# Moving parts of the weight decoding of a windowed attention + FFN kernel from ScalarE and VectorE to GpSimd

## The chip, the cores and the metric

One core of one Trainium2 chip. The metric is the device time of one execution in microseconds; three executions of the kernel before gave 1013.37, 1012.92 and 1012.87 us (median 1012.92).

## What is computed

An attention over 8 batches and 8 heads (512 local tokens that see a window of 32 to each side and 32 global tokens that see everything; head dimension 64), whose output of 4608 x 512 goes through a feed-forward layer (512 to 2048 to 512). Everything is float32.

```
s_ll = scale * q_l @ k_l^T, masked to |i - j| <= 32
a_l  = softmax([scale * q_l @ k_g^T, s_ll]);   out_l = a_l @ [v_g, v_l]
out_g = softmax(scale * q_g @ [k_g, k_l]^T) @ [v_g, v_l]
x = rows of [out_g, out_l], heads side by side (4608 x 512)
h = x @ w_in;  r = max(h, 0);  g = s * (r * r) + b;  out = g @ w_out
```

## The kernel before

Matrix products are made of split numbers: an operand m is cut into a high part `hi` (m rounded to float32r) and a low part `lo = m - hi`, and three float32r products (hi hi, hi lo, lo hi) are summed. ScalarE mostly makes the high part (a cast), VectorE or GpSimd the low part (a subtraction).

The program is one loop over steps j. Step j does one head-half of the attention, `scores` (or `scores32`, the unsplit form of the first 16 steps), softmax, transposes and the product with v; and, ten steps behind (LAG), one piece of the feed-forward layer: `ffn_in` (L517: 24 matmuls of 256 columns into `ps_h`; then Relu on ScalarE, L523, and squaring on VectorE, L524; then g's high part on ScalarE, L531, and its low part on VectorE, L532) and a step later `ffn_out` (L549: 12 matmuls of 512 columns into `acc`). There are 128 attention steps and 136 feed-forward pieces.

The two weight matrices come as 16 chunks, both matrices together 2 x 1024 numbers per partition for a chunk: `weight_load` brings chunk k as 64-bit integers (the bits of float64 numbers, 2 x 512 KB, tile `wst`), and `weight_chunk` decodes it at step k into `w_all`, by halves: the first half is columns 0 to 511 (w_in's), the second 512 to 1023 (w_out's). For each half `weight_words` (L152 on) issues six instructions of 512 columns on 128 partitions: ScalarE takes the upper bits of the low word (L160, tile `wup`) and the scaled high word (L161); VectorE shifts (L164) and adds (L165), which gives the float32 number m in `wst`; ScalarE casts it to the high part (L168), and VectorE subtracts for the low part (L169). Feed-forward piece m reads chunks 2 (m mod 8) and the one behind it, so the last chunk is wanted at step 17. After that the weights stay in `w_all` for the whole run. `wst` has four buffers, shared with other tiles (tags xs0, xs1 and two of kq); chunk k's buffer is loaded again, or used as `kq` or `xs`, when both low parts of the chunk that was there have been made.

Each engine works through its instructions in order. That order isn't the order of the code: a scheduler lays all instructions out beforehand by its own estimates of their lengths, so an edit at one place can move instructions everywhere. Loads go out in order on SyncE's queue. GpSimd has no decoding to do before the change: in the first 93 us it makes the masks and one small tile (`qgs`, L366), and from then on the low parts of q, v and of every other k (L206, L214, L204, L461).

Of the kernel before, what the change touches and what calls it, by code (L numbers as in the profile page):

```python
# [65 lines left out]
def f32(ap):  # L66
    return ap.bitcast(F32)
# [3 lines left out]
def window_attention_then_ffn(ctx: ExitStack, tc: tile.TileContext, qd, qg, kw, vw, vg, qz, qgz, vz, w_in, w_out, sv, bv, out):  # L71
    nc = tc.nc
# [37 lines left out]
    for tile_, c0, shift in ((mask_low, 32, -32), (mask_mid, 32, 0), (mask_high, 0, 32)):  # L110
        nc.gpsimd.memset(tile_, 0.0)
        part = tile_[:, c0:c0 + 192]
        for sign, base in ((1, -shift), (-1, 64 + shift)):
            nc.gpsimd.affine_select(
                out=part, in_=part, pattern=[[sign, 192]], compare_op=ALU.is_ge,
# [31 lines left out]
    def weight_chunk(k):  # L147
        st = staged.pop(k)
        n = 2 if k < BY_HALVES else 1
        for i in range(n):  # L150
            c = 1024 // n
            weight_words(k, st[:, 2 * c * i:2 * c * (i + 1)], slice(c * i, c * (i + 1)))  # L152

    def weight_words(k, st, at):
        words = st.rearrange("p (n w) -> p n w", w=2)
        low, high = words[:, :, 0], words[:, :, 1]
        n = at.stop - at.start
        pool, tag = ((ops, "vsg"), (sb, "pg"))[(k + at.start // 512) % 2]
        up = pool.tile([P, n], I32, tag=tag, name=f"wup{k}_{at.start}", bufs=1)
        nc.scalar.activation(out=up, in_=low.bitcast(U32), func=AF.Copy, scale=2.0**-29)  # L160
        nc.scalar.activation(  # L161
            out=low.bitcast(F32), in_=high.bitcast(F32), func=AF.Prelu, scale=2.0**-112, alpha=2.0**32,
        )
        nc.vector.tensor_scalar(out=low, in0=low, scalar1=3, scalar2=None, op0=ALU.logical_shift_left)  # L164
        nc.vector.tensor_tensor(out=low, in0=low, in1=up, op=ALU.add)  # L165
        m = low.bitcast(F32)
        hi, lo = (w_all[:, i, k].rearrange("p w c -> p (w c)")[:, at] for i in range(2))
        nc.scalar.copy(out=hi, in_=m)  # L168
        nc.vector.tensor_sub(out=lo, in0=m, in1=f32(hi))  # L169


    NS = B * 2 * H
# [426 lines left out]
    for j in range(NM + LAG + 2):  # L599
# [27 lines left out]
        m = j - LAG if LAG <= j < NM + LAG else None  # L627
# [91 lines left out]
```

## Time and profile before

| | before |
|---|---|
| median of 3 executions | 1012.92 us |
| the profiled execution | 1013.71 us, span of its trace 1011.9 us |
| TensorE busy | 996.1 us (98%) |
| VectorE busy | 809.4 us (80%) |
| ScalarE busy | 707.6 us (70%) |
| GpSimd busy | 289.4 us (29%) |
| mean granted TensorE clock | 0.997 of 2.4 GHz |

In the traces PE is TensorE's matmuls, PEld its weight loads, DVE VectorE, ACT ScalarE, POOL GpSimd, SP SyncE. The matmuls are pipelined and their ends modelled, so a full PE column says that matmuls followed one another, not that TensorE was at its peak. A row of grouped instructions gives the busy time and the mean of one, and behind the bar the engine's idle time before them with what ended it.

### The profile page before, as it was taken

The numbers are of one execution on the slowest core, as the hardware profiler recorded it, in microseconds if no ns is written. First come the engines' busy times: TensorE is split into PE (matmuls) and PEld (weight loads), VectorE is DVE, ScalarE is ACT, GpSimd is POOL, SyncE is SP. The second block draws the span as 40 slices with busy tenths as digits, with TensorE's granted clock in tenths as the row PEclk, the third lists the DMA queues.
The fourth block names the chain that finished last, engine by engine and source line by source line (L and its number), as shares of the span: only waits on it lengthen the run. The fifth ranks groups of instructions, "written<-read, shape, count | busy, mean of one in ns | idle before, by whom it ended". The sixth has DMA issues, their size and how long they took to land.

```text
span 1011.9 us, 20076 instructions
## 1 busy us (share of the span) xinstructions
PE 996.1 (98%) x6946; PEld 906.9 (90%) x6948; DVE 809.4 (80%) x2111; ACT 707.6 (70%) x1817; POOL 289.4 (29%) x366
## 2 busy tenths in 40 slices
PE   9799999999999999999999999999999999999998
PEld 5599899999999999999999999999999999999887
DVE  6999879988789788888789779988799788964322
ACT  7999767868677667868677667867678667743222
POOL 1001433424244224424234223424234223401000
PEclk9999999999999999999999999999999999999999
DMA  9765312313122212313132112312132112101000
GB/s 327 266 229 182 98 48 63 108 34 96 47 88 69 65 48 62 97 42 90 47 99 69 54 59 62 97 42 87 44 104 70 53 55 65 62 1 49 23 22 21
DMA packets 63557, 82.05 MB, mean 81 GB/s; under 512 B 7648, under 2 KB 50656, under 8 KB 63456
## 3 DMA queue, kind: packets, MB, share of 16 engines
q1 hardware_dynamic: 63168, 79.72, 25.2%
q8 instruction: 55, 0.90, 0.4%
q10 hardware_dynamic: 288, 1.05, 0.3%
q14 instruction: 46, 0.38, 0.1%
HBM read 71.30 MB, written 9.44 MB: 80 GB/s over the span
## 4 chain that ended last, share of the span: by engine, by line
PE 91%; ACT 5%; DVE 2%; DMA 1%; issue 0%
PE ps_h L517 35%; PE acc L549 35%; PE ps_s L375 5%; PE ps_o L403 4%; PE turned L311 3%; PE turned L313 3%; PE ps_og L469 2%; PE ps_g L382 1%; PE warm L105 1%; DMA rk<-in_kw 1%; ACT wst L161 1%; ACT wup L160 1%; ACT w_all L168 1%; ACT sm L231 1%; PE turned L447 1%; PE ps_s L286 1%
## 5 line engine op out<-in xcount | busy, mean ns | idle before, releaser
L517 PE MATMUL ps_h<-xst,w_all 128*128 128x256 f32 x3264 | 437.5, 281 | 1.8 <-ACT xst L502 0.7
L549 PE MATMUL acc<-w_all,g 128*128 128x512 f32 x1632 | 422.0, 396 | 0.0
L517 PEld LDWEIGHTS ps_h<-xst,w_all 128*128 128x128 f32 x3264 | 407.6, 189 | 9.3 <-ACT xst L489 1.1
L549 PEld LDWEIGHTS acc<-w_all,g 128*128 128x128 f32 x1632 | 289.8, 188 | 49.8
L214 POOL TENSOR_TENSOR vs<-rv,vs 128x192 fp32r<-128x192 f32 x112 | 70.7, 631 | 291.0 <-ACT vs L213 289.9
L524 DVE SCALAR_TENSOR_TENSOR r<-ps_h,s_t,r 128x512 f32<-128x512 f32 x136 | 101.4, 746 | 53.7 <-ACT r L523 52.2
L231 ACT ACTIVATE sm<-sm,nm 128x224 f32<-128x224 f32 x256 | 121.5, 478 | 32.5 <-DVE nm L225 31.3
L206 POOL TENSOR_TENSOR kq<-rq,kq 128x256 fp32r<-128x256 f32 x112 | 92.8, 828 | 169.2 <-ACT kq L205 160.3
L532 DVE SCALAR_TENSOR_TENSOR g<-r,b_t,g 128x512 fp32r<-128x512 f32 x136 | 112.0, 824 | 35.6 <-ACT g L531 31.1
L531 ACT ACTIVATE g<-r,b_t 128x512 fp32r<-128x512 f32 x136 | 98.6, 725 | 52.0 <-DVE r L524 51.9
L523 ACT ACTIVATE r<-ps_h 128x512 f32<-128x512 f32 x136 | 81.3, 598 | 67.7 <-PE ps_h L517 58.4
L241 DVE TENSOR_SCALAR sm<-sm,nm 128x224 f32<-128x224 f32 x256 | 92.2, 402 | 3.9
L461 POOL TENSOR_TENSOR vsg<-rvg,vsg 128x320 fp32r<-128x320 f32 x64 | 56.9, 910 | 107.1 <-ACT vsg L460 107.1
L375 PE MATMUL ps_s<-kq 128*128 128x224 f32 x448 | 73.7, 275 | 2.3 <-DVE nm L225 2.3
L375 PEld LDWEIGHTS ps_s<-kq 128*128 128x128 f32 x448 | 67.3, 190 | 8.9 <-ACT pt L328 2.5
L392 ACT CAST pt<-turned 128x416 fp32r<-128x416 f32 x112 | 57.5, 514 | 23.5 <-PE turned L313 22.8
L393 DVE TENSOR_TENSOR pt<-turned,pt 128x416 fp32r<-128x416 f32 x112 | 65.4, 584 | 6.9 <-ACT pt L392 6.2
L386 ACT COPY tg<-ps_g 32x256 f32<-32x256 f32 (+1 forms) x112 | 42.2, 377 | 33.9 <-PE ps_g L382 31.4
L387 DVE TENSOR_TENSOR sg<-ps_g,tg 32x256 f32<-32x256 f32 (+1 forms) x112 | 48.2, 430 | 20.7 <-ACT tg L386 15.9
L311 PE MATMUL turned<-ident,sm 128*96 128x128 f32 (+1 forms) x256 | 63.9, 274 | 0.0
L313 PE MATMUL turned<-ident,sm 128*128 128x128 f32 x256 | 63.2, 273 | 0.0
L403 PE MATMUL ps_o<-pt,vs 128*128 128x256 f32 x336 | 62.6, 295 | 0.0
(79 smaller groups left out, 1288.0 us busy)
## 6 DMA issues: line engine op xcount, KB each, us to landing
rq<-in_qd SPq DMA_DIRECT2D x112, 128.0 KB, 2.1
rk<-in_kw SPq DMA_DIRECT2D x64, 176.0 KB, 2.3
rv<-in_vw SPq DMA_DIRECT2D x112, 96.0 KB, 1.9
rvg<-in_vg SPq DMA_DIRECT2D x32, 320.0 KB, 3.0
out<-o SPq DMA_DIRECT2D x34, 256.0 KB, 2.2
wst<-in_w_in SPq DMA_DIRECT2D x15, 512.0 KB, 4.4
wst<-in_w_out SPq DMA_DIRECT2D x15, 512.0 KB, 5.5
rv<-in_vz SPq DMA_DIRECT2D x16, 192.0 KB, 4.2
```

The costliest lines, as they stand in the source:

```text
L206: nc.gpsimd.tensor_sub(out=qs[:, 1, :], in0=rq, in1=f32(qs[:, 0, :]))
L231: nc.scalar.activation(out=p, in_=p, func=AF.Exp, bias=nm[:, blk:blk + 1], scale=-1.0, accum_out=ss[:, blk:blk + 1],)
L241: nc.vector.tensor_scalar(out=p, in0=p, scalar1=ss[:, blk:blk + 1], scalar2=1.0, op0=ALU.mult, op1=ALU.mult,)
L311: nc.tensor.transpose(out=p_t[0:n, s0:s0 + P], in_=sm[:, c0:c0 + n], identity=ident)
L313: nc.tensor.transpose(out=p_t[:, o0:o0 + P], in_=sm[:, c0:c0 + P], identity=ident)
L375: nc.tensor.matmul(p_s[:, W * blk:W * blk + W], lhsT=qs[:, a, blk * P:(blk + 1) * P], rhs=ks[:, KEYS[blk]], start=(a == 0), stop=(a == 1),)
L403: nc.tensor.matmul(p_o[:, :, q], lhsT=vs[0:n, c], rhs=pt[0:n, :, o], start=(c == 0), stop=(c == 1))
L517: nc.tensor.matmul(p_h[:, k], lhsT=wi[:, a, f, c], rhs=xs[:, e, c, :], start=(n == 0), stop=(n == 11),)
L524: nc.vector.scalar_tensor_tensor(out=r, in0=p_h, scalar=s_t, in1=r, op0=ALU.mult, op1=ALU.mult)
L531: nc.scalar.activation(out=g[:, 0], in_=r, func=AF.Identity, bias=b_t)
L532: nc.vector.scalar_tensor_tensor(out=g[:, 1], in0=r, scalar=b_t, in1=f32(g[:, 0]), op0=ALU.add, op1=ALU.subtract,)
L549: nc.tensor.matmul(oacc[t][i], lhsT=g[:, a, k, i * P:(i + 1) * P], rhs=wo[:, e, f, :], start=(pr == 0 and n == 0), stop=(pr == 7 and n == 5),)
```

## The change

In `weight_words` the first half of every chunk (`at.start` is 0) has its high part made by GpSimd (`tensor_copy`) in place of ScalarE, and its low part by VectorE as before; the second half has its high part made by ScalarE as before and its low part by GpSimd in place of VectorE. So 16 of the 32 casts leave ScalarE, 16 of the 32 subtractions leave VectorE, and GpSimd gets 32 instructions of 128 x 512.

```diff
         m = low.bitcast(F32)
         hi, lo = (w_all[:, i, k].rearrange("p w c -> p (w c)")[:, at] for i in range(2))
-        nc.scalar.copy(out=hi, in_=m)
-        nc.vector.tensor_sub(out=lo, in0=m, in1=f32(hi))
+        if not at.start:
+            nc.gpsimd.tensor_copy(out=hi, in_=m)
+        else:
+            nc.scalar.copy(out=hi, in_=m)
+        (nc.gpsimd if at.start else nc.vector).tensor_sub(out=lo, in0=m, in1=f32(hi))
```

Line numbers behind the edit grow by 3: the copy on GpSimd is L169, the cast on ScalarE L171, both subtractions L172, and what was L206, L225, L524 is L209, L228, L527.

GpSimd's order. In each row stands the operation, the tile written and the tiles read. Before, behind the masks (L114), the first things that it does are `qgs` and the low parts for step 16:

```order
L114 AFFINE_SELECT mask_high_63<-mask_high_63 128x192
L366 TENSOR_TENSOR qgs1_1134<-rqg1_1032,qgs1_1134 128x8x32
L206 TENSOR_TENSOR kq16_1097<-rq16_1016,kq16_1097 128x256
L204 TENSOR_TENSOR kq16_1097<-rk16_1014,kq16_1097 64x352
L206 TENSOR_TENSOR kq16_1097<-rq17_1102,kq16_1097 128x256
```

With the change the 32 decoding instructions stand ahead of and among these; the rows for chunks 11 to 15 (CAST is the copy of a first half, TENSOR_TENSOR on `w_all` the subtraction of a second half):

```order
L169 CAST w_all_60<-wst11_601 128x512
L172 TENSOR_TENSOR w_all_60<-wst11_601,w_all_60 128x512
L172 TENSOR_TENSOR w_all_60<-wst12_664,w_all_60 128x512
L169 CAST w_all_60<-wst12_664 128x512
L169 CAST w_all_60<-wst13_735 128x512
L172 TENSOR_TENSOR w_all_60<-wst13_735,w_all_60 128x512
L172 TENSOR_TENSOR w_all_60<-wst14_833,w_all_60 128x512
L169 CAST w_all_60<-wst14_833 128x512
L209 TENSOR_TENSOR kq16_1097<-rq16_1016,kq16_1097 128x256
L207 TENSOR_TENSOR kq16_1097<-rk16_1014,kq16_1097 64x352
L209 TENSOR_TENSOR kq16_1097<-rq17_1102,kq16_1097 128x256
L169 CAST w_all_60<-wst15_915 128x512
```

Two subtractions or two copies now follow each other, and the low parts for step 16 stand between those of chunks 14 and 15.

VectorE's order around chunk 12 (`wst12`); ISA on `wst` is the addition (L165), ISA on `sm` the masked row maximum of the softmax. Before:

```order
L164 TENSOR_SCALAR wst12_664<-wst12_664 128x512
L234 TENSOR_SCALAR nm15_1124<-nm15_1124 128x2
L165 ISA wst12_664<-wst12_664,wup12_512_843 128x512x2
L235 RECIPROCAL nm15_1124<-nm15_1124 128x2
L169 TENSOR_TENSOR w_all_60<-wst11_601,w_all_60 128x512
L241 TENSOR_SCALAR sm15_1123<-sm15_1123,nm15_1124 128x224 x2
L524 SCALAR_TENSOR_TENSOR r4_1072<-ps_h4_1047,s_t_90,r4_1072 128x512
L169 TENSOR_TENSOR w_all_60<-wst12_664,w_all_60 128x512
L164 TENSOR_SCALAR wst12_664<-wst12_664 128x512
L165 ISA wst12_664<-wst12_664,wup12_0_836 128x512x2
L532 SCALAR_TENSOR_TENSOR g4_1075<-r4_1072,b_t_91,g4_1075 128x512
```

With the change:

```order
L164 TENSOR_SCALAR wst12_664<-wst12_664 128x512
L165 ISA wst12_664<-wst12_664,wup12_0_836 128x512x2
L527 SCALAR_TENSOR_TENSOR r3_973<-ps_h3_948,s_t_90,r3_973 128x512
L237 TENSOR_SCALAR nm14_1038<-nm14_1038 128x2
L238 RECIPROCAL nm14_1038<-nm14_1038 128x2
L244 TENSOR_SCALAR sm14_1037<-sm14_1037,nm14_1038 128x224 x2
L164 TENSOR_SCALAR wst13_735<-wst13_735 128x512
L172 TENSOR_TENSOR w_all_60<-wst12_664,w_all_60 128x512
```

One subtraction for each chunk is left, and between the addition that feeds GpSimd's copy and the subtraction that reads the copy the scheduler has put five other rows (six instructions).

SyncE's order of loads, from chunk 4's on, before:

```order
L265 DMA rk4_243<-in_kw 128x352
L271 DMA rq4_245<-in_qz 128x256
L145 DMA wst4_247<-in_w_in 128x1024
L145 DMA wst4_247<-in_w_out 128x1024
L271 DMA rq5_292<-in_qz 128x256
```

With the change the two loads of chunk 4, which also wait for GpSimd now (it releases the buffer), stand ahead of step 4's keys and queries:

```order
L145 DMA wst4_247<-in_w_in 128x1024
L145 DMA wst4_247<-in_w_out 128x1024
L268 DMA rk4_243<-in_kw 128x352
L274 DMA rq4_245<-in_qz 128x256
L274 DMA rq5_292<-in_qz 128x256
```

## Rows read from the trace of the kernel before

**Rows 1.** The page: the span; busy time, share and instructions of each engine.

```profile
span 1011.9 us, 20076 instructions
PE 996.1 (98%) x6946; PEld 906.9 (90%) x6948; DVE 809.4 (80%) x2111; ACT 707.6 (70%) x1817; POOL 289.4 (29%) x366
```

**Rows 2.** Busy time of each engine by stretch: the stretch (us), its length, then busy us (and instructions) of PE, PEld, DVE, ACT, POOL; granted clock, DMA share, GB/s.

```profile
24.00:52.00 28.00, 22.06 (x130) 16.59 (x131) 26.31 (x92) 27.39 (x69) 0.00 (x0) 1.00 0.78 265
52.00:96.00 44.00, 44.00 (x300) 40.42 (x300) 42.30 (x108) 43.69 (x99) 3.24 (x4) 1.00 0.66 223
96.00:108.00 12.00, 9.45 (x62) 8.29 (x61) 11.87 (x26) 11.03 (x27) 5.64 (x8) 1.00 0.26 76
108.00:200.00 92.00, 92.00 (x659) 85.59 (x660) 79.24 (x208) 68.22 (x183) 34.61 (x42) 0.98 0.26 79
```

**Rows 3.** The same for 24 to 108 us in one piece.

```profile
24.00:108.00 84.00, 75.51 (x489) 65.30 (x490) 80.47 (x224) 82.10 (x193) 8.89 (x11) 1.00 0.64 216
```

**Rows 4.** Pieces of the chain that ended last, 86 to 100 us: start, us on the chain, engine, tile, line.

```profile
86.27 0.54 ACT w_all L168
...
90.85 0.58 ACT wst L161
...
95.93 0.75 DVE w_all L169
```

**Rows 5.** Waits in 24 to 108 us: the waiting engine, tile and line, what it waited for, us in total, times, longest.

```profile
PE ps_s L375 <- DVE nm L225: 2.3, 1, 2.3
...
DVE w_all L169 <- ACT w_all L168: 0.2, 1, 0.2
```

**Rows 6.** VectorE's largest groups that read nothing but SBUF, in 24 to 108 us, and ScalarE's casts of the decoding: count | busy us, mean ns | idle before.

```profile
L169 DVE TENSOR_TENSOR w_all<-wst,w_all 128x512 fp32r<-128x512 f32 x27 | 18.8, 702 | 0.3 <-ACT w_all L168 0.2
L165 DVE CUSTOM_DVE_ANT_0 wst<-wst,wup 128x1024 uint16<-128x1024 uint16 x26 | 18.5, 713 | 0.2
L164 DVE TENSOR_SCALAR wst<-wst 128x512 int32<-128x512 int32 x25 | 10.6, 425 | 1.6 <-ACT wst L161 1.1
L241 DVE TENSOR_SCALAR sm<-sm,nm 128x224 f32<-128x224 f32 x28 | 9.5, 381 | 0.0
...
L532 DVE SCALAR_TENSOR_TENSOR g<-r,b_t,g 128x512 fp32r<-128x512 f32 x7 | 5.2, 748 | 0.4 <-ACT g L531 0.2
...
L168 ACT CAST w_all<-wst 128x512 fp32r<-128x512 f32 x26 | 17.3, 666 | 0.4 <-DVE wst L165 0.3
```

**Rows 7.** Two successive instructions on VectorE in order of time: start, length in us.

```profile
101.55 0.68 DVE L169 TENSOR_TENSOR w_all<-wst,w_all 128x512 fp32r<-128x512 f32 x1
102.15 0.69 DVE L165 CUSTOM_DVE_ANT_0 wst<-wst,wup 128x1024 uint16<-128x1024 uint16 x1
```

**Rows 8.** GpSimd's subtractions over the whole run: count, duration in ns least/median/greatest, first and last start.

```profile
L214 POOL TENSOR_TENSOR vs<-rv,vs x112: 589/602/1056, 99.4 to 894.9; 128x192 fp32r<-128x192 f32 x112
...
L206 POOL TENSOR_TENSOR kq<-rq,kq x112: 724/741/1313, 93.3 to 876.3; 128x256 fp32r<-128x256 f32 x112
...
L461 POOL TENSOR_TENSOR vsg<-rvg,vsg x64: 870/910/1062, 104.0 to 939.4; 128x320 fp32r<-128x320 f32 x64
```

**Rows 9.** GpSimd's instructions with one input in SBUF, at the start: start, length in us.

```profile
1.20 0.29 POOL masks.py:199 TENSOR_SCALAR_AFFINE_SELECT ident<-ident 128x128 f32<-128x128 f32 x1
...
1.69 0.34 POOL L114 TENSOR_SCALAR_AFFINE_SELECT mask_low<-mask_low 128x192 bf16<-128x192 bf16 x1
```

**Rows 10.** GpSimd in order of time, 93 to 107 us: the first instructions that it runs beside a full VectorE.

```profile
93.35 0.85 POOL L206 TENSOR_TENSOR kq<-rq,kq 128x256 fp32r<-128x256 f32 x1 [27.32 <-ACT kq L205]
94.28 1.10 POOL L204 TENSOR_TENSOR kq<-rk,kq 64x352 fp32r<-64x352 f32 x1
95.46 1.07 POOL L206 TENSOR_TENSOR kq<-rq,kq 128x256 fp32r<-128x256 f32 x1
...
103.97 1.92 POOL L461 TENSOR_TENSOR vsg<-rvg,vsg 128x320 fp32r<-128x320 f32 x2 [0.68 <-ACT vsg L460]
105.85 0.76 POOL L206 TENSOR_TENSOR kq<-rq,kq 128x256 fp32r<-128x256 f32 x1
```

**Rows 11.** VectorE at the same times, and (last row) the pair L241 at a time without GpSimd beside it.

```profile
93.64 0.94 DVE L204 TENSOR_TENSOR kq<-rk,kq 64x352 fp32r<-64x352 f32 x1
94.61 1.32 DVE L165 CUSTOM_DVE_ANT_0 wst<-wst,wup 128x1024 uint16<-128x1024 uint16 x1
95.86 1.22 DVE L169 TENSOR_TENSOR w_all<-wst,w_all 128x512 fp32r<-128x512 f32 x1
...
104.22 1.81 DVE L241 TENSOR_SCALAR sm<-sm,nm 128x224 f32<-128x224 f32 x2
106.06 0.93 DVE L204 TENSOR_TENSOR kq<-rk,kq 64x352 fp32r<-64x352 f32 x1
...
109.49 0.57 DVE L241 TENSOR_SCALAR sm<-sm,nm 128x224 f32<-128x224 f32 x2
```

**Rows 12.** Least/median/greatest duration (ns) over the run of VectorE instructions: two that read only SBUF, and one that reads PSUM (`ps_h`).

```profile
L532 DVE SCALAR_TENSOR_TENSOR g<-r,b_t,g x136: 733/752/1365, 61.1 to 1004.0; 128x512 fp32r<-128x512 f32 x136
...
L204 DVE TENSOR_TENSOR kq<-rk,kq x56: 518/604/1122, 93.6 to 874.5; 64x352 fp32r<-64x352 f32 x56
...
L524 DVE SCALAR_TENSOR_TENSOR r<-ps_h,s_t,r x136: 730/746/754, 56.3 to 1002.5; 128x512 f32<-128x512 f32 x136
```

**Rows 13.** Waits of SyncE's queue, 0 to 110 us, longest in total.

```profile
SPq L145 <- DVE w_all L169: 9.2, 4, 4.9
```

## The prediction

> **What bounds the kernel now.** I read the busy times first: TensorE 98%, VectorE 80%, ScalarE 70%, GpSimd 29% of the span [rows 1]. That mean says that TensorE sets the time, and for most of the run it does. But all 16 chunks are decoded in the first 108 us, so I read the stretches next [rows 2]. From 108 us on TensorE is always busy, VectorE has 14% and ScalarE 26% of the time to spare, and nothing of the change happens there. From 24 to 108 us it is the other way round: over these 84 us ScalarE is busy 82.10 and VectorE 80.47, GpSimd only 8.89 [rows 3]. The chain that ended last runs there through ScalarE's decoding instructions until 91 us and then through VectorE's [rows 4], so what the two can get through sets how fast the steps follow. The reader should see as well that TensorE is nearly supplied: it idles 5.9 us in 24 to 52, nothing in 52 to 96, and 2.55 us in 96 to 108 [rows 2], of which 2.3 is one wait for a row maximum from VectorE [rows 5]. Work that comes later than now makes TensorE idle; work that comes earlier can save no more than these 8.5 us.
>
> So everything is decided in 84 us, by VectorE, ScalarE and what GpSimd does to VectorE.
>
> **The change, part by part.** All sums are against the profiled execution, 1013.71 us (span 1011.9), 0.8 above the median of 1012.92; I add the difference to the median. Of the 32 decoded halves some 27 fall into the stretch (27 subtractions, 26 casts) [rows 6], so I count 13.5 of each of the four kinds; the first chunks meet engines with free time.
>
> *ScalarE loses 13 casts.* On the chain one stands for 0.54 us [rows 4]: 13 x 0.54 = 7.0 us less of 82.1. ScalarE is then at 75 of 84 and no longer the bound.
>
> *VectorE loses 13.5 subtractions.* One holds the engine from 101.55 to 102.15, 0.60 us, the recorded 0.68 being overlapped [rows 7]: 13.5 x 0.60 = 8.1 us less.
>
> *GpSimd gains 13.5 subtractions of 512 columns.* The least durations of its own ones are 589, 724 and 870 ns for 192, 256 and 320 columns [rows 8]: (870 - 589) / 128 = 2.2 ns a column, so 0.87 + 192 x 0.0022 = 1.29 us.
>
> *GpSimd gains 13.5 copies.* No row shows one. From below: its instructions with one SBUF input take 0.29 us for 128 columns and 0.34 for 192 [rows 9], 0.8 ns a column, so 0.29 + 384 x 0.0008 = 0.60 us. From above: the subtraction's 1.29. I take 0.80, nearer the lower, because a copy reads one tensor as those do. The Trainium skill's GPSIMD Engine Reference (Engine selection) has one-input operations run roughly at line rate; no row here shows it for float32 copies, and taken with the lower end it would bring the sum below down by 1.2 us.
>
> Together 13.5 x (1.29 + 0.80) = 28.2 us on GpSimd, with 8.9 there already: it has room.
>
> *What GpSimd takes from VectorE.* This is the term that decides. Before 93 us GpSimd runs one instruction beside the full VectorE; then the trace shows what happens. In 93.35 to 96.53 GpSimd runs three subtractions, 3.02 us in sum [rows 10]; VectorE's three instructions of that time take 0.94, 1.32 and 1.22 us [rows 11] where L204 needs 0.52 at the least [rows 12] and the other two some 0.69: 1.59 us more, 0.53 for each us of GpSimd's. In 103.97 to 106.61 it runs 2.68 us; VectorE's pair L241 takes 1.81 where it takes 0.57 without GpSimd, and L204 0.93 for 0.52 [rows 10 to 12]: 1.65 us more, 0.62 for each. Instructions that read only SBUF stretch to twice their length in this kernel, one that reads PSUM, L524, never (730 to 754 ns) [rows 12]. I take 0.57, times the share of VectorE's time that can be hit: L169, L165, L164, L241 and L532 are 62.6 of 80.5 us [rows 6], and without half of L169 53.2 of 71.1, 0.75. So 28.2 x 0.57 x 0.75 = 12.1 us. Ends: no loss at all if GpSimd always finds VectorE in PSUM-fed work, 0; and GpSimd's whole duration with the copy at 1.29: 13.5 x 2.58 x 0.75 = 26.1.
>
> The Trainium skill speaks against this change: SBUF — State Buffer (SBUF: two separate sides) says that a VectorE instruction with two SBUF inputs or in a two-port mode and a GpSimd instruction exclude each other for the whole instruction. The rows agree on who is hit and disagree on how much, 0.57 and not 1, since part of what is recorded for GpSimd is not the hold.
>
> *Sum.* VectorE: 80.5 - 8.1 + 12.1 = 84.5 us. It had 3.5 us idle in the stretch and shares its work with ScalarE in chains, so I let it keep them: 88.0 us where there were 84, **4 us later**. Nothing behind 108 us can win this back, since TensorE has no idle time there. 1012.92 + 4.1 = **1017 us**.
>
> *What is moved with it.* VectorE's subtraction of a first half now waits for GpSimd's copy where it waited for ScalarE's cast (0.2 us in sum [rows 5]). In the new order six instructions stand between the addition that feeds the copy and that subtraction (around chunk 12), more than 2 us of work for a 0.8 us copy: I cost this wait at nothing, and if the copy is late, behind it wait the row maxima that TensorE needs. A chunk's buffer is now released by GpSimd too, and SyncE's queue already waits 9.2 us for such releases [rows 13]; the loads are issued steps ahead of their decoding, so nothing again; if one comes late, the longest such wait, 4.9 us, is the price. Chunk 4's loads stand ahead of step 4's keys now: 1 MB at 265 GB/s [rows 2], 4 us later keys, while decoding work arrives 4 us earlier for engines that are full either way. Zero; its price uncovered is those 4 us once.
>
> **The rivals.** About 0.2%, 2 us, is what a measurement of this kernel can tell from no change.
>
> *The relief counts, the loss doesn't (faster, chance 0.21).* If the scheduler's order puts GpSimd's work beside PSUM-fed work, and the copy is at 0.60, VectorE loses little: 13.5 x 1.89 = 25.5 us of GpSimd's at a third of 0.57 make 5 us, 80.5 - 8.1 + 5 = 77.4, and ScalarE's 75 fits too. The stretch could shorten by 6 us, and TensorE's recoverable idle time is 2.55 at its end and some of the 5.9 before: I put it at 4 to 5 us, 1008.5. For it: ScalarE bounds until 91 us and is relieved for certain. Against: 0.53 and 0.62 were measured in this very stretch. The point from which it decides: the loss must stay 2 us under the relief of 8.1, 6.1 / 28.2 = 0.22 for each us of GpSimd's, where I count 0.57 x 0.75 = 0.43.
>
> *Whole instructions exclude each other (slower, 0.16).* 28.2 x 0.75 = 21.2 us lost: 80.5 - 8.1 + 21.2 + 3.5 = 97.1, 13 us later, 1026. For it: the longest cases are about double [rows 12]; against: both bursts. This is the rule of the Trainium skill's SBUF — State Buffer (SBUF: two separate sides) taken at its word.
>
> *GpSimd's order makes others wait (slower, 0.12).* A subtraction for a second half stands in GpSimd's queue ahead of the next copy and waits for ScalarE's cast; the copy behind it is late, and so are VectorE's subtraction, and the row maxima behind that. One such wait of a subtraction's length, 1.29 us, at every second chunk, 7 x 1.29 = 9 us, less what the spare ScalarE time gives back, on top of 4: some 11, 1024.
>
> *Nothing to see (same, 0.16).* The loss just equals the relief (8.1 us, 0.29 for each us of GpSimd's), or TensorE, busy throughout 52 to 96 us, has enough queued to hide the delay: 1013. That the change does not do what it says can be left out: the 32 instructions stand in GpSimd's order.
>
> **How the numbers follow.** My case, 2 to 8 us slower, has 0.35. Faster is 0.21, within 0.2% 0.16, slower 0.35 + 0.16 + 0.12 + 0.02 for worse mishaps = 0.63. My case's own range is 1015 to 1021. The range that holds 8 in 10 takes in the faster rival's 1008.5 and the slower ones' 1024 and 1026, with 2 us beyond for the copy's price (13.5 x 0.49 x 0.43 = 2.8): 1007 to 1029.
>
> **What would show it.** Right: GpSimd some 37 us busy in 24 to 108 us, its copies 0.6 to 1.0 us, its subtractions 1.3 to 1.5; L165, L164, L172 and L244 with means well over now and L527 unchanged; ScalarE with idle time before 92 us; the first 108 us of work ending some 4 us later, and from there on the same pace. Wrong: VectorE's means as before and TensorE idle less than 8.5 us (faster); VectorE idle behind GpSimd's copies for several us (its order, not the shared access, costs); or a loss, but with TensorE never idle, which would mean that the clock or the order of its matmuls changed.

## The result

The changed kernel takes 1020.73 us (median, 1019.17 to 1021.11) where the kernel before takes 1013.14: ratio **1.0066, 95% interval 1.0054 to 1.0079**, by the ratio some 6.7 us slower. 1017.0 was forecast, slower, in a range of 1007 to 1029. The direction and the kind of loss came out as forecast; the deciding term was 2 us too small, and another 2 us, late in the run, were not foreseen.

In the profile after, line numbers up to L167 are the same and later ones three higher: L169 is GpSimd's copy, L171 ScalarE's cast, L172 the subtraction on either engine, L244 the scaling that was L241, L237 the one that was L234, L535 the one that was L532, L527 the one that was L524. The page's span and busy times (answer to [rows 1]):

```profile
span 1019.3 us, 20130 instructions
...
PE 998.7 (98%) x6948; PEld 906.7 (89%) x6948; DVE 814.9 (80%) x2095; ACT 701.1 (69%) x1801; POOL 325.1 (32%) x398
```

Busy time by stretch (answer to [rows 2, 3]; PE, PEld, DVE, ACT, POOL, then granted clock, DMA share, GB/s):

```profile
24.00:108.00 84.00, 73.75 (x456) 62.41 (x455) 82.47 (x203) 72.98 (x169) 36.10 (x34) 0.98 0.63 213
24.00:52.00 28.00, 20.94 (x113) 14.39 (x111) 27.11 (x77) 24.14 (x59) 9.72 (x10) 1.00 0.79 269
52.00:96.00 44.00, 41.55 (x273) 38.00 (x272) 43.52 (x108) 39.23 (x89) 17.19 (x15) 0.96 0.66 226
96.00:108.00 12.00, 11.26 (x74) 10.02 (x73) 11.83 (x21) 9.60 (x23) 9.19 (x9) 1.00 0.12 37
```

The four engines tell the story. GpSimd went from 8.89 to 36.10 us. ScalarE was relieved, from 82.10 to 72.98. VectorE lost half its subtractions and is *fuller* than before, 82.47 for 80.47: no work of its own did that. And TensorE, which had no idle time in 52 to 96 us, now has 2.45 there.

The groups of 24 to 108 us show who got longer (answer to [rows 6]; count | busy us, mean ns | idle before):

```profile
L165 DVE CUSTOM_DVE_ANT_0 wst<-wst,wup 128x1024 uint16<-128x1024 uint16 x26 | 20.8, 805 | 0.2
L244 DVE TENSOR_SCALAR sm<-sm,nm 128x224 f32<-128x224 f32 x28 | 14.7, 564 | 0.2
L172 DVE TENSOR_TENSOR w_all<-wst,w_all 128x512 fp32r<-128x512 f32 x14 | 11.7, 833 | 0.0
L164 DVE TENSOR_SCALAR wst<-wst 128x512 int32<-128x512 int32 x25 | 10.8, 437 | 0.0
L237 DVE TENSOR_SCALAR nm<-nm 128x2 f32<-128x2 f32 x14 | 6.3, 452 | 0.0
...
L535 DVE SCALAR_TENSOR_TENSOR g<-r,b_t,g 128x512 fp32r<-128x512 f32 x6 | 4.9, 811 | 0.0
L527 DVE SCALAR_TENSOR_TENSOR r<-ps_h,s_t,r 128x512 f32<-128x512 f32 x6 | 4.4, 740 | 0.0
...
L172 POOL TENSOR_TENSOR w_all<-wst,w_all 128x512 fp32r<-128x512 f32 x13 | 18.4, 1415 | 28.1 <-ACT w_all L171 28.1
L169 POOL CAST w_all<-wst 128x512 fp32r<-128x512 f32 x14 | 11.6, 831 | 21.5 <-DVE wst L165 14.9 <-DVE gm L435 3.2 <-DVE nm L237 2.0
```

Against the means of before, the growth is 26 x (805 - 713) = 2.4 us on L165, 28 x (564 - 381) = 5.1 on L244, 14 x (833 - 702) = 1.8 on L172, 14 x (452 - 162) = 4.1 on L237 (162 ns is the mean of the same group, then L234, before), 0.3 on L164 and 0.4 on L535: **14.1 us in these six** (13.8 over all of VectorE's groups, since some got a little shorter). L527, which reads PSUM, did not grow. A mean hides how it happens; two stalls in order of time (start, length) show it:

```profile
80.27 1.39 POOL L172 TENSOR_TENSOR w_all<-wst,w_all 128x512 fp32r<-128x512 f32 x1 [2.40 <-ACT w_all L171]
80.41 1.64 DVE L244 TENSOR_SCALAR sm<-sm,nm 128x224 f32<-128x224 f32 x2
...
83.41 1.37 POOL L172 TENSOR_TENSOR w_all<-wst,w_all 128x512 fp32r<-128x512 f32 x1 [1.75 <-ACT w_all L171]
83.64 1.69 DVE L165 CUSTOM_DVE_ANT_0 wst<-wst,wup 128x1024 uint16<-128x1024 uint16 x1
85.26 0.73 DVE L527 SCALAR_TENSOR_TENSOR r<-ps_h,s_t,r 128x512 f32<-128x512 f32 x1
85.40 0.67 POOL L169 CAST w_all<-wst 128x512 fp32r<-128x512 f32 x1 [0.62 <-DVE wst L165]
...
86.33 0.58 DVE L244 TENSOR_SCALAR sm<-sm,nm 128x224 f32<-128x224 f32 x2
```

An L165 that starts 0.23 us behind a subtraction of GpSimd's takes 1.69 us and ends 0.55 after it, where it takes 0.69 by itself; the pair L244 takes 1.64 beside a subtraction and 0.58 beside nothing. L527 passes beside a copy untouched.

The waits (us in total, times, longest; 24 to 116 us) show what this did to TensorE and what GpSimd itself waits for (answer to [rows 5]):

```profile
POOL w_all L172 <- ACT w_all L171: 28.1, 12, 4.7
POOL w_all L169 <- DVE wst L165: 14.9, 9, 2.6
...
PE ps_s L289 <- DVE nm L228: 4.3, 3, 2.1
```

TensorE waits for row maxima from VectorE. Among VectorE's waits none for a copy of GpSimd's is listed.

To place the loss I compare when the pieces of the feed-forward part start: ScalarE's `r<-ps_h`, 136 of them, one list for each kernel. Start in the profiled run minus the start of the same piece before, in us (piece 5 is at 82 us before, 9 at 118, 13 at 143, 53 at 430):

| kernel | 1 | 5 | 7 | 9 | 13 | 25 | 53 | 113 | ratio (95%) |
|---|---|---|---|---|---|---|---|---|---|
| after | 5.5 | 8.2 | 12.5 | 1.7 | 5.5 | 5.5 | 7.6 | 7.5 | 1.0066 (1.0054 to 1.0079) |
| subtractions alone, second halves | -0.5 | -0.6 | 3.7 | 0.7 | 0.8 | 4.9 | 5.5 | 5.6 | 1.0051 (1.0038 to 1.0064) |
| subtractions alone, first halves | 4.0 | 3.1 | 4.6 | 1.9 | 2.8 | 2.7 | 3.2 | 3.2 | 1.0021 (1.0012 to 1.0030) |
| copies alone | 5.3 | 6.8 | 9.8 | 4.3 | 5.7 | 5.7 | 5.4 | 5.7 | 1.0037 (1.0024 to 1.0051) |
| load without relief | 4.0 | 7.3 | 8.8 | 13.1 | 13.1 | 13.3 | 14.5 | 15.2 | 1.0129 (1.0113 to 1.0146) |
| work left out | 16.2 | 16.5 | 16.2 | 9.2 | 12.3 | 12.3 | 12.0 | 12.3 | 1.0131 (1.0114 to 1.0148) |
| old order + 18 subtractions | -0.2 | 12.8 | 13.4 | 12.0 | 12.2 | 12.2 | 13.4 | 13.6 | 1.0132 (1.0117 to 1.0148) |
| old order + 16 copies | -0.5 | 2.6 | 4.3 | 2.8 | 3.0 | 3.0 | 4.3 | 4.4 | 1.0028 (1.0017 to 1.0038) |
| old order + 36 fills | -0.4 | 0.0 | 0.5 | 0.5 | 0.7 | 0.7 | 1.3 | 1.4 | 1.0010 (1.0001 to 1.0019) |
| old order, VectorE relieved | 0.7 | 0.8 | 0.7 | -1.8 | -1.7 | -1.7 | -1.0 | -1.0 | 0.9989 (0.9978 to 1.0000) |
| after, all fills | 1.9 | 4.4 | 7.6 | -3.8 | 0.3 | 0.3 | 1.0 | 1.1 | 0.9995 (0.9985 to 1.0005) |
| after, copies real | 2.3 | 3.9 | 7.5 | -3.9 | 0.2 | 0.2 | 0.5 | 0.6 | 1.0000 (0.9989 to 1.0011) |
| after, subtractions real | 3.1 | 5.5 | 9.5 | -1.6 | 2.5 | 2.5 | 3.2 | 3.2 | 1.0034 (1.0022 to 1.0046) |

Two things are needed to read it. Up to piece 12 a row also shows that pieces stand elsewhere among the attention's steps in a new order; from piece 13 to the fortieth or so most rows are steady.

The other is the clock. In most profiled runs TensorE's granted clock is at its lower level, 1.2 of 2.4 GHz, for some time in the first 128 us: 0.61 in the mean of 108 to 112 us before (TensorE busy 9.45 of the 12 us ahead of it), 0.60 in 56 to 60 after (1.55 of the 4 us ahead of it), 0.57 in 40 to 44 in "after, all fills". While TensorE is busy that is worth (1 - 0.61) x 4 = 1.6 us. Before, after, the two with fills or copies in after's order, "old order + 36 fills" and the subtractions of the first halves have 1.6 to 1.7 us of it each, so their differences stand. The three rows "old order + 16 copies", "old order, VectorE relieved" and "after, subtractions real" have none: from piece 9 on they stand 1.6 us too low, which gives 4.6, -0.1 and 4.1 at piece 13. Five rows have more, counted in the same way: 3.4 us the subtractions of the second halves, 5.2 "old order + 18 subtractions", 6.8 each the copies alone, the load without relief and the work left out. Where TensorE is the bound, that is time lost on top of what VectorE loses; where VectorE is, it costs less, as the 18 subtractions show below.

### The profile page after: what moved, and what is told of

Read it like the earlier page. It is cut to its first block, busy times and chain, and to the rows that moved or that the text cites. A ratio compares the mean times of both kernels' runs of the same rounds, so it can differ in the third digit from the quotient of the medians.

```text
span 1019.3 us, 20130 instructions
## 1 busy us (share of the span) xinstructions
PE 998.7 (98%) x6948; PEld 906.7 (89%) x6948; DVE 814.9 (80%) x2095; ACT 701.1 (69%) x1801; POOL 325.1 (32%) x398
## 4 chain that ended last, share of the span: by engine, by line
PE 87%; DVE 6%; ACT 3%; DMA 2%; issue 1%; ACTq 0%; DVEq 0%
PE acc L552 34%; PE ps_h L520 34%; PE ps_s L378 4%; PE ps_o L406 4%; PE turned L314 2%; PE turned L316 2%; PE ps_og L472 2%; PE ps_g L385 1%; DMA wst<-in_w_out 1%; DMA out<-o 1%; DVE wst L165 1%; DVE sm L244 1%; PE turned L450 1%; DVE wst L164 1%; DVE w_all L172 1%
## 5 line engine op out<-in xcount | busy, mean ns | idle before, releaser
L234 ACT ACTIVATE sm<-sm,nm 128x224 f32<-128x224 f32 x256 | 121.6, 477 | 35.7 <-DVE nm L228 34.4
L527 DVE SCALAR_TENSOR_TENSOR r<-ps_h,s_t,r 128x512 f32<-128x512 f32 x136 | 101.4, 746 | 55.9 <-ACT r L526 54.4
L535 DVE SCALAR_TENSOR_TENSOR g<-r,b_t,g 128x512 fp32r<-128x512 f32 x136 | 112.2, 825 | 35.8 <-ACT g L534 31.3
L209 POOL TENSOR_TENSOR kq<-rq,kq 128x256 fp32r<-128x256 f32 x112 | 93.1, 831 | 137.5 <-ACT kq L208 129.3
L244 DVE TENSOR_SCALAR sm<-sm,nm 128x224 f32<-128x224 f32 x256 | 98.6, 427 | 4.2
```

Source lines behind the costliest of these rows:

```text
L209: nc.gpsimd.tensor_sub(out=qs[:, 1, :], in0=rq, in1=f32(qs[:, 0, :]))
L234: nc.scalar.activation(out=p, in_=p, func=AF.Exp, bias=nm[:, blk:blk + 1], scale=-1.0, accum_out=ss[:, blk:blk + 1],)
L244: nc.vector.tensor_scalar(out=p, in0=p, scalar1=ss[:, blk:blk + 1], scalar2=1.0, op0=ALU.mult, op1=ALU.mult,)
L527: nc.vector.scalar_tensor_tensor(out=r, in0=p_h, scalar=s_t, in1=r, op0=ALU.mult, op1=ALU.mult)
L535: nc.vector.scalar_tensor_tensor(out=g[:, 1], in0=r, scalar=b_t, in1=f32(g[:, 0]), op0=ALU.add, op1=ALU.subtract,)
```

## Experiments

The theory: GpSimd's reading of SBUF holds up VectorE's SBUF-fed instructions, by the forecast 0.43 us for each of its own. The rivals: waits for GpSimd's parts; the new order of the program; and that relief alone would pay.

**One part at a time, and both without relief.** These went first. The program's order is made anew for each of them.

Subtractions alone:

```diff
-        nc.vector.tensor_sub(out=lo, in0=m, in1=f32(hi))
+        (nc.gpsimd if at.start else nc.vector).tensor_sub(out=lo, in0=m, in1=f32(hi))
```

> Only the second halves' subtractions on GpSimd, all casts on ScalarE. Shared access (GpSimd's instruction lengthens VectorE's SBUF-fed ones): VectorE loses 13.5 subtractions (8.1 us) and pays 13.5 x 1.4 x 0.45 = 8.5 us; ScalarE stays as it was. So 1013 to 1014 us, VectorE's L165 and softmax scaling with longer means. Waits (GpSimd's queue makes others late): GpSimd still waits for ScalarE's casts and still releases the weight buffers, so most of the loss stays, 1017 to 1020.

Copies alone:

```diff
-        nc.scalar.copy(out=hi, in_=m)
+        if not at.start:
+            nc.gpsimd.tensor_copy(out=hi, in_=m)
+        else:
+            nc.scalar.copy(out=hi, in_=m)
```

> Only the first halves' casts on GpSimd as copies, all subtractions on VectorE. Shared access: VectorE has all its work and pays 13.5 x 0.8 x 0.45 = 4.9 us on top; ScalarE is relieved of 7 us: 1014 to 1018 us. Waits: VectorE's subtraction waits for the copy in GpSimd's queue, where nothing stands ahead of it now: 1010 to 1013, since ScalarE's relief counts.

The load without relief, beside the kernel before's own work:

```diff
+    scratch = const.tile([P, 480], BF16, name="scratch")
...
+        if not at.start:
+            nc.gpsimd.tensor_copy(out=scratch, in_=m[:, 0:480])
+        else:
+            nc.gpsimd.tensor_sub(out=scratch, in0=m[:, 0:480], in1=f32(hi)[:, 0:480])
```

> The kernel before, with 32 instructions on GpSimd beside it (16 copies of m, 16 subtractions, 480 columns), whose results nobody reads. Shared access: VectorE's work of 80.5 us grows by 0.45 x 28 = 12 to 14 us with nothing taken off it: 1023 to 1028. Waits: nobody waits for these results but the reloading of a weight buffer: 1013 to 1015.

The relief without load; it leaves out the 32 moved parts, and two fills stand in for them ahead of the masks:

```diff
+    nc.gpsimd.memset(f32(w_all[:, 0, :, 0]), 0.5)
+    nc.gpsimd.memset(f32(w_all[:, 1, :, 1]), 0.5)
...
-        if not at.start:
-            nc.gpsimd.tensor_copy(out=hi, in_=m)
-        else:
+        if at.start:
             nc.scalar.copy(out=hi, in_=m)
-        (nc.gpsimd if at.start else nc.vector).tensor_sub(out=lo, in0=m, in1=f32(hi))
+        else:
+            nc.vector.tensor_sub(out=lo, in0=m, in1=f32(hi))
```

> The 32 moved instructions are made by nobody: the first halves' high parts and the second halves' low parts stay at a constant written at the start. What is left is the relief alone, no GpSimd work beside VectorE. Shared access: the loss is gone, VectorE has 72 and ScalarE 75 us of work in the 84: faster than before by 3 to 7 us, 1006 to 1010. If the stage is held by something else (TensorE's order, loads), no gain: 1012 to 1014.

Measured: 1019.48, 1018.43, 1028.15 and 1027.15 us, with 1014.72 for the kernel before in the same series. The load without relief came out in size as the theory had it, 13.1 us later at piece 13. The theory accounts for the 8.8 at piece 7: VectorE's groups grow by 11.7 us in 24 to 108 us (each count times its mean less the mean before), and 2.8 of that come out of its idle time. Most of the rest falls in 116 to 128 us, where the granted clock is 0.72, 3.4 us that the kernel before doesn't lose.

The last was a badly built experiment: its two fills took 6.9 and 7.2 us ahead of the masks that the first softmaxes need, and all its pieces come late by that; it tells nothing of relief.

The totals of the two single parts miss the theory. The subtractions lose nothing up to piece 16 (165 us; -0.7), as the theory has it, since VectorE's groups grow by 6.2 us for a relief of 8.1; but then they lose 5 us by piece 25, long after the last moved part (105 us). The copies alone cost 5.7, though VectorE's groups grow by only 3.4: the granted clock is 0.92 in the mean of 24 to 108 us where it was 1.00, and that can be up to 5.1 us of it. So an edit's new order moves such totals by several us in other ways than through VectorE. That called for experiments in which the order stays.

**Subtractions of the first halves**, the mirror of the first one, to see what order alone does:

```diff
-        (nc.gpsimd if at.start else nc.vector).tensor_sub(out=lo, in0=m, in1=f32(hi))
+        (nc.vector if at.start else nc.gpsimd).tensor_sub(out=lo, in0=m, in1=f32(hi))
```

> The mirror of the kernel in which GpSimd subtracts in the second halves alone: here it subtracts in the first halves, ScalarE makes every copy. The same work and the same shared access, in another order of the program. Shared access: the feed-forward pieces up to the 16th come within 1.5 us of the kernel before. If the loss of the second-half kernel between 165 and 185 us was a matter of order, it is not there at the same place here and the total differs from 1019.5 by over 1 us (1012 to 1017 likeliest); if it is a late cost of the moved subtractions themselves, it comes again, 1018 to 1021.

1016.09 us. The late loss is not there (2.8 at piece 13, 2.7 at piece 25); the same moved work costs, by the ratios, 3.0 us less than in the second halves. The order is worth that much by itself; what in the order does it was not followed up. That the stage would come within 1.5 us was a miss: 2.8.

**Load in the old order.** Four engines keep the kernel before's order row for row (with the copies up to 97 us only: there, behind the last copy, VectorE, ScalarE and TensorE each do something in another order); GpSimd gets work behind `qgs` that nobody waits for, between 66 and 93 us. `q` is qgs split into 16 blocks of 32 columns.

```diff
+    scratch = const.tile([P, 14, SG], BF16, name="scratch")
...
+    for _ in range(18):
+        nc.gpsimd.tensor_sub(out=scratch, in0=q[:, 0:14, :], in1=q[:, 2:16, :])
```

> The kernel before with one thing added: 18 subtractions of 128x448 on GpSimd, which read qgs and write a scratch tile that nobody reads, in its queue between qgs and the low parts of the next keys (about 66 to 92 us). The order of the four other engines stays row for row that of the kernel before, so the placing of work can cost nothing here. Shared access: 18 x 1.2 to 1.4 = 22 to 25 us of GpSimd in a stretch in which VectorE is full, x 0.43 to 0.57 = 9 to 14 us later at the first pieces of the feed-forward part; VectorE's shift of L164, its subtraction of L169 and its scaling of L241 grow by 20 to 60% in the mean over that stretch and the copies from PSUM of L524 do not; total 1022 to 1027. Waits in GpSimd's queue or another order: nobody waits for the added work, total 1013 to 1015.

```diff
...
+    for _ in range(16):
+        nc.gpsimd.tensor_copy(out=scratch, in_=q[:, 0:14, :])
```

> As the kernel with 18 added subtractions in the old order, but with 16 one-input copies of 128x448 from qgs to the scratch tile in their place (some 0.65 to 0.75 us each, 10.4 to 12 us of GpSimd between 66 and 90 us). If a copy takes from VectorE what a subtraction takes, 0.55 us for each us of GpSimd's: 5.7 to 6.6 us later at the first pieces, total 1019 to 1021. If a copy takes only what the fills took, under 0.1 for each us: at most 1.5 us later, total 1013.5 to 1015.5. In between: a share by how long it holds the access.

```diff
...
+    nc.gpsimd.tensor_copy(out=scratch, in_=q[:, 0:14, :])
+    for _ in range(36):
+        nc.gpsimd.memset(scratch, 0.0)
```

> As the kernel with 18 subtractions, but in their place one copy and 36 fills of 128x448 (estimate 0.4 us each by the fills of the experiment with left-out work, 6.9 us for 8192 columns; some 15 us of GpSimd in all), which write and read nothing. Shared access, if GpSimd's reading is what blocks VectorE: 1 us later at the first pieces at most, total 1013 to 1015. Shared access, if any access blocks: 15 x 0.43 to 0.57 = 6 to 9 us later, total 1019 to 1023. Waits or order: 1013 to 1015.

1026.87, 1016.92 and 1014.70 us, with 1014.0 to 1014.1 for the kernel before. With the subtractions no order changed and nobody waits for the scratch tile, and they still cost 12 to 13 us: this is neither order nor waits, VectorE's own instructions are longer. The three kinds that the expectation names grew by 33 to 171%, where 20 to 60 was expected. The groups in 64 to 94 us, count | busy us, mean ns | idle before, first the kernel before:

```profile
L169 DVE TENSOR_TENSOR w_all<-wst,w_all 128x512 fp32r<-128x512 f32 x11 | 7.3, 681 | 0.0
L165 DVE CUSTOM_DVE_ANT_0 wst<-wst,wup 128x1024 uint16<-128x1024 uint16 x10 | 6.9, 691 | 0.1
L164 DVE TENSOR_SCALAR wst<-wst 128x512 int32<-128x512 int32 x11 | 4.7, 424 | 0.8 <-ACT wst L161 0.6
...
L524 DVE SCALAR_TENSOR_TENSOR r<-ps_h,s_t,r 128x512 f32<-128x512 f32 x4 | 3.0, 744 | 0.1
L241 DVE TENSOR_SCALAR sm<-sm,nm 128x224 f32<-128x224 f32 x8 | 2.5, 357 | 0.0
```

with 18 subtractions (lines one higher):

```profile
L166 DVE CUSTOM_DVE_ANT_0 wst<-wst,wup 128x1024 uint16<-128x1024 uint16 x5 | 6.1, 1226 | 0.0
L165 DVE TENSOR_SCALAR wst<-wst 128x512 int32<-128x512 int32 x5 | 5.7, 1148 | 0.0
L170 DVE TENSOR_TENSOR w_all<-wst,w_all 128x512 fp32r<-128x512 f32 x6 | 5.4, 907 | 0.0
L242 DVE TENSOR_SCALAR sm<-sm,nm 128x224 f32<-128x224 f32 x6 | 5.3, 924 | 0.0
...
L525 DVE SCALAR_TENSOR_TENSOR r<-ps_h,s_t,r 128x512 f32<-128x512 f32 x2 | 1.5, 738 | 0.0
...
L629 POOL TENSOR_TENSOR scratch<-qgs 128x448 bf16<-128x448 f32 x18 | 24.4, 1356 | 1.4
```

with 16 copies:

```profile
L166 DVE CUSTOM_DVE_ANT_0 wst<-wst,wup 128x1024 uint16<-128x1024 uint16 x9 | 7.1, 793 | 0.1
L170 DVE TENSOR_TENSOR w_all<-wst,w_all 128x512 fp32r<-128x512 f32 x10 | 6.7, 679 | 0.0
L165 DVE TENSOR_SCALAR wst<-wst 128x512 int32<-128x512 int32 x9 | 5.1, 565 | 0.0
L242 DVE TENSOR_SCALAR sm<-sm,nm 128x224 f32<-128x224 f32 x8 | 3.6, 487 | 0.0
...
L629 POOL CAST scratch<-qgs 128x448 bf16<-128x448 f32 x16 | 12.2, 760 | 1.0
```

with 36 fills:

```profile
L170 DVE TENSOR_TENSOR w_all<-wst,w_all 128x512 fp32r<-128x512 f32 x11 | 7.3, 678 | 0.0
L166 DVE CUSTOM_DVE_ANT_0 wst<-wst,wup 128x1024 uint16<-128x1024 uint16 x10 | 6.9, 689 | 0.1
L165 DVE TENSOR_SCALAR wst<-wst 128x512 int32<-128x512 int32 x11 | 5.6, 510 | 0.2 <-ACT wst L162 0.2
L242 DVE TENSOR_SCALAR sm<-sm,nm 128x224 f32<-128x224 f32 x8 | 4.0, 538 | 0.0
...
L630 POOL MEMSET scratch<- 128x448 bf16 x36 | 18.5, 514 | 2.1
```

The price for each us of GpSimd's time, beside a full VectorE, from the start of piece 7 (95 us before, ahead of any change of order): 13.4 / 24.4 = **0.55 for a subtraction**, 4.3 / 12.2 = **0.35 for a copy**, 0.5 / 18.5 = **0.03 for a fill**. That is what came late. VectorE's groups themselves grow by 14.6, 4.4 and 3.4 us in this stretch: 0.60, 0.36 and 0.18. For subtractions the two differ by VectorE's idle time, 1.4 of the 30 us before and none now, so the lower clock at 80 to 88 us (0.57 in the mean) has no part in the 13.4. A fill, then, is not free for VectorE: some 1 of its 3.4 us came out of that idle time, and the rest hardly made the pieces late.

The fills were expected to take 0.4 us and took 0.51. They lengthen L165 and L242, which have one tensor as input, and the short L235 (491 ns for 164), which has one too; the instructions with two, L166 and L170, stay at their length.

The Trainium skill, SBUF — State Buffer (SBUF: two separate sides), has the pair of ports locked for a whole instruction, against a VectorE instruction with two SBUF inputs only if GpSimd's instruction reads SBUF. On the second part the fills agree. The copies, which do read, agree for L166 (793 ns for 691); the subtraction L170 keeps its 679 ns, but of its ten only three ran beside a copy, and some L170 pass at 0.68 us beside subtractions too, so that settles nothing.

**The changed kernel's order kept, its load taken away.** Every engine's order and wait stay; GpSimd's 16 copies and 16 subtractions become fills of the same columns, so the relief and the queue stay and the reading goes. The edit is made in the finished list of instructions (`blank` is a fill):

```diff
...
+    for block in nc.main_func.blocks:
+        for i in block.instructions:
...
+            if str(i.engine).endswith("Pool") and type(i).__name__ in ("InstTensorCopy", "InstTensorTensor") and i.outs[0].ap[-1][1] == 512:
+                block.instructions[block.instructions.index(i)] = _copy.replace(
+                    blank, name=i.name, outs=[_copy.replace(i.outs[0], dtype=F32)], sync_info=i.sync_info, debug=i.debug)
```

> The changed kernel, with every engine's order and every wait kept, but each of GpSimd's 16 copies and 16 subtractions turned into a fill of the same 512 columns with zeros: it leaves out the high part of each first half and the low part of each second half of the feed-forward weights. Shared access: VectorE's loss is gone and its relief of 8.1 us is left, so the feed-forward pieces come 0 to 8 us earlier than in the kernel before, total 1005 to 1014. Order of the program or waits for GpSimd's parts: the 5.5 us of the changed kernel stay nearly whole, total 1017 to 1021.

Then with one of the two kinds of instruction in that condition:

```diff
-            if str(i.engine).endswith("Pool") and type(i).__name__ in ("InstTensorCopy", "InstTensorTensor") and i.outs[0].ap[-1][1] == 512:
+            if str(i.engine).endswith("Pool") and type(i).__name__ in ("InstTensorTensor",) and i.outs[0].ap[-1][1] == 512:
```

> The changed kernel in its own order, GpSimd's 16 copies left as they are and its 16 subtractions turned into fills with zeros (the low part of each second half is left out). Shared access: some 11 us of reading on GpSimd are left of 36; at most 0.55 x 11 = 6 us are lost on VectorE, of which the idle time that it has with fills alone (8 of 84 us) takes the larger part: total 1014 to 1017.5, VectorE's L165 and L244 between their means with fills and those of the changed kernel. Waits of VectorE for GpSimd's copies: these are all still there, total 1019 to 1021.

```diff
-            if str(i.engine).endswith("Pool") and type(i).__name__ in ("InstTensorCopy", "InstTensorTensor") and i.outs[0].ap[-1][1] == 512:
+            if str(i.engine).endswith("Pool") and type(i).__name__ in ("InstTensorCopy",) and i.outs[0].ap[-1][1] == 512:
```

> The changed kernel in its own order, GpSimd's 16 subtractions left and its 16 copies turned into fills with zeros (VectorE's low part then carries the whole weight of a first half). Shared access: 13.5 x 1.4 = 19 us of reading are left, 0.55 x 19 = 10 us lost on VectorE less its idle time: total 1016 to 1020, more than with the copies alone. Waits of VectorE for GpSimd's copies: a fill is shorter than a copy, total 1013 to 1015.

1013.92, 1014.41 and 1017.62 us, with 1014.07 to 1014.37 for the kernel before: with fills as fast as that, with the copies too, with the subtractions 0.34% slower. Order is out as the cause of the loss, for it is the same in all three. So are the waits for GpSimd's copies, which the second has in full. Waits for its subtractions are shorter behind a fill (0.55 us for 1.42), and SyncE's queue waits 6.4 us for the subtractions in the changed kernel; but no engine there waits for a weight load in 24 to 116 us. The stretch 24 to 108 us, with fills, with copies, with subtractions:

```profile
24.00:108.00 84.00, 76.80 (x486) 66.07 (x486) 75.95 (x213) 75.33 (x177) 24.07 (x36) 0.98 0.65 221
```

```profile
24.00:108.00 84.00, 76.25 (x484) 65.84 (x484) 77.67 (x213) 75.02 (x177) 27.51 (x35) 0.98 0.65 220
```

```profile
24.00:108.00 84.00, 74.61 (x473) 63.09 (x472) 81.96 (x207) 73.51 (x171) 35.32 (x36) 1.00 0.65 218
```

VectorE is busy 75.95, 77.67, 81.96 and, with both, 82.47 of 84. The first two leave it idle time and cost nothing; the last two don't, and cost. What GpSimd takes is free until VectorE's relief is used up. VectorE's groups grow by 4.7, 5.4, 12.8 and 13.8 us in these four kernels; the prices of 0.60, 0.36 and 0.18 from the old order, times GpSimd's time in each kind, give 2.8, 5.3, 12.9 and 15.2.

**Relief alone in the old order.** VectorE's second-half subtractions become fills on VectorE in the same way. Their mean is 485 ns for the 702 of before, not the half that was expected.

```diff
...
+            if "w_all" in str(getattr(o, "memref", "")) and type(i).__name__ == "InstTensorTensor" and o.offset % 1024:
+                block.instructions[block.instructions.index(i)] = _copy.replace(
+                    blank, name=i.name, engine=i.engine, outs=[_copy.replace(o, dtype=F32)], sync_info=i.sync_info, debug=i.debug)
```

> The kernel before, every engine's order and wait kept, but VectorE's 16 subtractions of second halves turned into fills with zeros on VectorE (the low part of each second half is left out). If VectorE's time is what sets the first 108 us: a fill is at most half a subtraction, so 13.5 x 0.3 us or more come off, 3 to 5 us of which TensorE's idle time after 96 us can give back 2.5: total 1009.5 to 1011.5. If the relief is worth nothing because TensorE is supplied from 52 to 96 us and waits for loads before: 1012.5 to 1014.5.

1012.70 us, 0.9989 (0.9978 to 1.0000). In the profiled run the pieces up to the eighth come no earlier (0.4 to 0.8 later), and the gain behind it is the clock drop that this run lacks. Of the 2.9 us taken off (13.5 x 0.217) the ratio shows 1.1, at most 2.2. ScalarE stays full in it:

```profile
24.00:108.00 84.00, 76.28 (x496) 66.15 (x495) 78.27 (x227) 83.13 (x195) 8.44 (x10) 1.00 0.65 213
```

So it says that VectorE's relief alone pays little, and how little it can't say closer than nothing to 2.2 us. Relief of both engines is what the changed order with fills shows, 0.9995.

No version that computes the whole result beats the kernel before.

## Why the prediction was right, and where it was not

*The load on GpSimd: right.* 37 us forecast, 36.10 measured; a subtraction 1.29 forecast, 1.415 in the mean (it is itself held up); a copy 0.80 forecast, 0.83 measured. *ScalarE's relief* of 7.0 is 9.1 of 82.1, part of it waiting: its cast L171 alone now waits 3.7 us for VectorE's L165.

*The deciding term: right in kind, mis-sized, and nearer than its parts.* The forecast took 12.1 us off VectorE, 28.2 us of GpSimd's at one price of 0.57 x 0.75 = 0.43 for both kinds of work; the groups show 14.1 for 30.0 us. The runs show 0.55 for a subtraction and 0.35 for a copy. With 18.4 and 11.6 us of them that is 10.1 + 4.1 = 14.2; that it meets the groups so closely is in part luck, for the growth itself in the same runs gives 15.2. The term that was mis-sized is the share of 0.75, by the rows left out of it: L237, 128 x 2 elements and 162 ns, was not counted as work that can be hit since it is only 2.3 us in all, and lost 4.1. A stall has GpSimd's length, not that of the instruction that is stalled: up to 1.29 us for one L237. The five rows that were counted lost 10.0, less than the 12.1, so two errors of opposite sign brought the term near. One of the five, L164, was to have a mean well over that of before, and grew by 3% only.

*The sum: right in form, with a condition.* 80.5 - 8.1 + loss, plus 3.5 of idle time, gave 88.0. With the measured 14.1 it is 90.0, 6 us later, 1019; the pieces settle 5.5 later. What it did not say is that relief by itself is worth nothing here: with fills in GpSimd's place VectorE loses 4.7 us, the formula would have the stage 3.4 us shorter, and it is at 0.3 later at piece 13, with VectorE idle for 8 of 84 us. So the 9 us that the changed kernel loses on top of that cost 5.2 (5.5 - 0.3), the rest having been taken from time that was free. The formula holds only while VectorE is the bound, which it names as the condition; its rival "the relief counts", 1008.5 and a chance of 0.21, is refuted by both runs with relief and little load. Of TensorE's 8.5 us of idle time, which it meant to win back in part, 7.2 are still there with fills (84 - 76.80). The chances of the slower cases add up to 0.65, not to the 0.63 that is given.

*The steps costed at nothing: held.* The run with copies left, in the same order, shows no loss, so VectorE's waits for GpSimd's copies cost nothing to be seen. SyncE waits for buffers longer (15.1 us behind VectorE's L172 in its first 125 us, longest 5.4, for [rows 13]'s 9.2, and 6.4 behind GpSimd's), and no engine waits for a weight load in 24 to 116 us; with fills, 12.1 us behind VectorE's L172 cost nothing to be seen. *The rival of GpSimd's order*, 1024, is refuted by the same runs. *The rival of whole instructions* has its single stalls right, 1.0 us on L165 and up to 1.29 for an L237 that takes 0.16 by itself, and the sum wrong: 21.2 us were counted with it and 14.1 lost. VectorE gets its turn between two of GpSimd's instructions and runs PSUM-fed work beside them, which fits, but how much each of the two makes is not shown. The forecast's own reason for less than the whole, that part of GpSimd's record is not the hold, is small: in the two stalls above VectorE's instructions, taken at their own lengths, began 0.14 and 0.19 us ahead of the record's end.

*What the forecast did not have.* "From there on the same pace" holds to 354 us and then fails: two steps of 1 us at 354 to 365 and at 411 us, in the profiled run (the table's 5.5 and 7.6). At the first ScalarE waits 1.9 us for an output transfer:

```profile
ACT r L526 <- DMA out<-o: 1.9, 1, 1.9
```

The kernels with other edits lose -0.3 to 1.3 us between pieces 25 and 53, most of them some 0.6, for 2.1 here, so part of it may lie in the one profiled run of before that all are compared with. Whether the changed order or chance made it 2 stays open; it is the difference between the 5.5 us that the runs explain and the 6.7 of the ratio. Open too is how much of the 0.3 with fills is an order that costs a little and a relief that gives it back: pieces 5 to 7 are 4.4 to 7.6 us late there and piece 9 is 3.8 early.

## What to carry to other kernels

Before work goes to GpSimd, ask what VectorE does at that time: here a two-input subtraction took 0.55 us from a full VectorE for each us of its own, a copy 0.35, a fill 0.03 (though 0.18 of VectorE's own time), and short SBUF-fed instructions pay as much for one meeting as long ones. Weigh that price against the relief only where the relieved engine is the bound, and in the stretch; relief beyond the next bound is a reserve that hides such losses, not a gain. And when an edit lets a scheduler make a new order, take the order for a suspect worth some us of its own: test the cause with the order held, and read the granted clock of each run before its pieces are compared.

## What was not expected of the hardware

The order of turns. Beside 18 subtractions back to back (7 shown, 1.44 us each; start, length):

```profile
69.92 10.08 POOL L629 TENSOR_TENSOR scratch<-qgs 128x448 bf16<-128x448 f32 x7
...
70.15 1.50 DVE L166 CUSTOM_DVE_ANT_0 wst<-wst,wup 128x1024 uint16<-128x1024 uint16 x1
71.58 0.15 DVE L436 RECIPROCAL gm<-gm 128x1 f32<-128x1 f32 x1
71.65 1.30 DVE L165 TENSOR_SCALAR wst<-wst 128x512 int32<-128x512 int32 x1
72.87 1.64 DVE L533 SCALAR_TENSOR_TENSOR g<-r,b_t,g 128x512 fp32r<-128x512 f32 x1
...
75.74 1.64 DVE L166 CUSTOM_DVE_ANT_0 wst<-wst,wup 128x1024 uint16<-128x1024 uint16 x1
77.31 1.11 DVE L235 TENSOR_SCALAR nm<-nm 128x2 f32<-128x2 f32 x1
78.33 0.68 DVE L170 TENSOR_TENSOR w_all<-wst,w_all 128x512 fp32r<-128x512 f32 x1
```

VectorE gets about one SBUF-fed instruction through for each of GpSimd's, of whatever length: they take 1.30 to 1.64 us for work that takes 0.42 to 0.75 by itself, and 1.11 for work of 0.16. One that comes right behind a held one can pass at its own length, as L170 in the last row (0.68). The reciprocal (0.15) is not held at all.

The Trainium skill's SBUF — State Buffer (SBUF: two separate sides) has whoever starts first keep the ports for the whole instruction. The single stalls here agree with that, to within the 0.2 us by which they end ahead of GpSimd's record; that the turns are why their sum does not reach GpSimd's whole time fits these rows and is not shown.
